# A three-stage kernel in split fp32 (attention, a rational expert layer, a gated layer): one operand of the rational moves to PSUM, weight casts of layer 1 move to GpSimd, and the order of work is ranked anew

## The chip, the core and the metric

The program runs on one core of a Trainium2 chip. A core has TensorE (matrix products, PE in the profile; its weight loads are PEld), VectorE (DVE), ScalarE (ACT), GpSimd (POOL), and SyncE (SP), which here issues every DMA. Each engine works through its own instructions in order. The metric is the device time in microseconds (us) of one execution. Before the change it is 624.5 us (median of three runs, 623.87 to 624.86).

## The reference, cut to what matters

```python
# q, k, v: 2 batches, 12 heads, 448 tokens, 64 per head; x has 896 tokens of 768
scores = where(causal, q @ k.T / 8, -1e9);  attn = softmax(scores);  x = attn @ v
# layer 1: 768 -> 2048 -> 768
h = x @ w_in
P = a[0] + a[1]*h + a[2]*h**2 + a[3]*h**3
Q = 1.0 + abs(b[0])*abs(h) + abs(b[1])*h**2
x = (P / (Q + 1e-6)) @ w_out
# layer 2: 768 -> 1536 -> 768
y = (sigmoid(x @ w_gate) * (x @ w_val)) @ w_out
```

The weights arrive as 64-bit floats. All of it is wanted at fp32 accuracy.

## The kernel before, in words

**Products.** Every large product is made of three passes in the type fp32r: a value is split into a rounded part ("hi") and the rest ("lo"), and hi·hi, hi·lo and lo·hi are summed in one PSUM bank. So each matrix multiplication of a tile of 128 x 448 (or 128 x 384) is a row of *units*, each of three matmuls (lines 228 to 230 for products with w_in, w_gate and w_val, lines 280 to 282 for products with w_out of layer 1, lines 340 to 342 for w_out of layer 2).

**Weights.** The generator `weight` (line 140) brings one *portion* of weights (128 x 768 values) through six stages: a DMA on SP, two ScalarE passes over the two halves of the 64-bit words (lines 152 and 156), a VectorE instruction that joins them to an fp32 value `val` (line 159, both inputs in SBUF), the cast of `val` to its hi part on ScalarE (line 165), and the subtraction that leaves the lo part on GpSimd (line 167). The buffers `raw` and `val` hold two portions each.

**Layer 1** is cut into four chunks c of 512 hidden values, for each of two batches b. `stage_in(c, b)` makes four tiles h{c}_{b}_{i} of six units each. Each tile is followed by `rational` (line 233): three ScalarE passes from the PSUM tile `ps` into the SBUF temporaries z, d and t (lines 238 to 240), three VectorE instructions (242 to 244), logarithm and exponential on ScalarE, which leave 1/Q in d (247, 248), three VectorE instructions (250 to 252), the cast to gh on ScalarE (254) and the subtraction to gl on GpSimd (256). The temporaries have two buffers each. `stage_out(c, b)` makes six tiles o{c}_{b}_{e} of four units, one unit for each of the chunk's four pairs gh, gl; VectorE adds each tile to a running sum in SBUF (line 290; in chunk 0 ScalarE copies it, line 288), and in the last chunk the sum is split again into xh and xl (294, 296).

**Layer 2** has six chunks: tiles gu and vu of six units, a gate (316 to 322), and 14 tiles z of two units per chunk, which VectorE adds up (line 350).

**PSUM.** The products go to banks of two pools, two banks in `ps_a` and, once the attention is over, six in `ps_b`. A tile takes the next bank of the ring and must wait until the tile that had it has been read.

**Order.** Nothing is scheduled on the chip. Each piece of work is a `Job` with an engine, an estimated cost, dependencies and a rank. `in_turn` (line 36) plays the jobs through with the estimated costs; whenever an engine is free in that play it takes, of the jobs that are ready, the one of lowest rank. The instructions of each engine are then written down in that order, for good. An engine that reaches an instruction too early waits in front of it, and everything behind it waits too. The numbers R_... (lines 519 to 524) shift the ranks of the attention's jobs, the dictionary `due` (line 616) gives the ranks of weights and follow-up work in the layers, and the list `order` (line 601) gives the order of the stages: in(0,0), out(0,0), in(0,1), in(1,0), out(0,1), in(1,1), out(1,0) and so on, so that an in-stage always stands between a stage's own in and out. The attention (12 pairs of heads) runs first on all engines; units of in(0,0), out(0,0) fill TensorE in between. The job `late` stands after the attention's last job: it frees the attention's memory and opens the second weight buffers and the pool `ps_b`.

Of the kernel before, what the change touches and what calls it, by code (L numbers as in the profile page):

```python
# [62 lines left out]

@with_exitstack
def tile_causal_attention__moe_rational__moe_glu(
# [535 lines left out]
    order = [("in", 0, 0), ("out", 0, 0), ("in", 0, 1)]  # L601
    for c in range(NCH):
        for b in range(B):
            if (c, b) != (0, 0):
                order.append(("out", c, b))
            if c + 1 < NCH:
                order.append(("in", c + 1, b))
    order += [("in2", 0, b) for b in range(B)]
    for c in range(NCH2):
        for b in range(B):  # L610
            order.append(("out2", c, b))
            if c + 1 < NCH2:
                order.append(("in2", c + 1, b))
# [1 line left out]
    due = {}
    pos = 1000.0
    for o in order:
        due[o] = pos
        pos += {
            "in": KC * NF * UNIT,  # L620
            "out": KC * NF * UNIT,
            "in2": 2 * KC * NF2 * UNIT,
            "out2": 2 * (ready[o[2] + 1] - ready[o[2]]) * NF2 * UNIT2,
        }[o[0]]
# [211 lines left out]
```

## Time and profile before

| | |
|---|---|
| median of three runs | 624.5 us |
| the profiled execution | 626.6 us, its span from the first to the last instruction 624.8 us |
| PE busy | 606.8 us, 97% of the span |
| DVE busy | 385.0 us, 62% |
| ACT busy | 382.5 us, 61% |
| POOL busy | 232.0 us, 37% |
| attention with its fill-in units | 0 to about 122.6 us |
| layer 1 from there, with the last sums | to about 355 us |
| layer 2 | the rest |

A share of the whole span is a mean over three stages that have different limits, so it does not tell what limits a stage. The windows of the trace tell that: the busy time of each engine in a stretch, and the clock that TensorE was granted in it (1.00 is full speed). A busy TensorE is not always a TensorE at its peak, since the ends of its matmuls are modelled; how many matmuls start in a stretch is the check on it.

### The profile page before, as it was taken

The numbers are of one execution on the slowest core, as the hardware profiler recorded it, in microseconds if no ns is written. First come the engines' busy times: TensorE is split into PE (matmuls) and PEld (weight loads), VectorE is DVE, ScalarE is ACT, GpSimd is POOL, SyncE is SP. The second block draws the span as 40 slices with busy tenths as digits, with TensorE's granted clock in tenths as the row PEclk, the third lists the DMA queues.
The fourth block names the chain that finished last, engine by engine and source line by source line (L and its number), as shares of the span: only waits on it lengthen the run. The fifth ranks groups of instructions, "written<-read, shape, count | busy, mean of one in ns | idle before, by whom it ended". The sixth has DMA issues, their size and how long they took to land.

```text
span 624.8 us, 8785 instructions
## 1 busy us (share of the span) xinstructions
PE 606.8 (97%) x3352; PEld 527.5 (84%) x3352; DVE 385.0 (62%) x659; ACT 382.5 (61%) x712; POOL 232.0 (37%) x155
## 2 busy tenths in 40 slices
PE   7998999999899999999996999999999999999997
PEld 5555566699799999999995999999999999999997
DVE  5776888838879999997896344435245245302314
ACT  6998988868877796878685276665516335121010
POOL 0332312245227444553446566435226135131110
PEclk9999999999999999999997999999999999999999
DMA  7643620153313341434050055434423232000004
GB/s 233 192 175 109 227 89 16 56 159 114 128 50 102 103 151 52 152 101 152 12 188 3 1 181 172 154 100 155 148 81 127 98 102 102 0 1 0 1 1 176
DMA packets 25641, 65.05 MB, mean 104 GB/s; under 512 B 1984, under 2 KB 3776, under 8 KB 25600
## 3 DMA queue, kind: packets, MB, share of 16 engines
q1 hardware_dynamic: 25600, 64.50, 31.6%
q8 instruction: 26, 0.43, 0.3%
q14 instruction: 15, 0.12, 0.1%
HBM read 61.74 MB, written 2.75 MB: 103 GB/s over the span
## 4 chain that ended last, share of the span: by engine, by line
PE 67%; DVE 19%; ACT 7%; issue 4%; DMA 2%; POOL 1%; DVEq 0%; POOLq 0%; ACTq 0%
PE vu L228 5%; PE vu L230 5%; PE gu L230 5%; PE gu L228 5%; PE gu L229 5%; PE vu L229 5%; PE z L340 5%; PE z L341 5%; PE z L342 5%; PE s L403 4%; DVE z_h L251 4%; PE p L443 4%; PE x L480 4%; DVE t_h L250 3%; DVE z_h L242 2%
## 5 line engine op out<-in xcount | busy, mean ns | idle before, releaser
L280 PE MATMUL o<-gh_h,oh_out 128*128 128x448 f32 x192 | 72.5, 378 | 4.6 <-ACT gh_h L254 4.6
L281 PE MATMUL o<-gl_h,oh_out 128*128 128x448 f32 x192 | 72.4, 377 | 4.1 <-POOL gl_h L256 4.1
L167 POOL TENSOR_TENSOR ol_out<-val_out,oh_out 128x768 fp32r<-128x768 f32 x28 | 55.2, 1983 | 48.3 <-ACT oh_out L165 40.2
L282 PE MATMUL o<-gh_h,ol_out 128*128 128x448 f32 x192 | 72.1, 375 | 0.0
L256 POOL TENSOR_TENSOR gl_h<-t_h,gh_h 128x448 fp32r<-128x448 f32 x32 | 43.2, 1349 | 76.8 <-ACT gh_h L254 62.9
L228 PE MATMUL h<-xh,wh_in 128*128 128x448 f32 x192 | 71.6, 373 | 0.0
L229 PE MATMUL h<-xl,wh_in 128*128 128x448 f32 x192 | 70.4, 367 | 1.0 <-POOL xl L501 1.0
L322 POOL TENSOR_TENSOR gl<-pr_u,gh 128x448 fp32r<-128x448 f32 x24 | 29.2, 1215 | 111.0 <-ACT gh L320 111.0
L230 PE MATMUL h<-xh,wl_in 128*128 128x448 f32 x192 | 70.1, 365 | 0.0
L318 DVE TENSOR_TENSOR pr_u<-sg_u,vu 128x448 f32<-128x448 f32 x24 | 14.8, 617 | 71.9 <-PE vu L230 59.6
L340 PE MATMUL z<-oh_out,gh 128*128 128x384 f32 x168 | 56.2, 334 | 0.0
L342 PE MATMUL z<-oh_out,gl 128*128 128x384 f32 x168 | 56.1, 334 | 0.0
L341 PE MATMUL z<-ol_out,gh 128*128 128x384 f32 x168 | 56.1, 334 | 0.0
L350 DVE TENSOR_TENSOR y<-y,z 128x384 f32<-128x384 f32 x70 | 37.9, 551 | 25.5 <-PE z L342 25.5
L425 ACT ACTIVATE e<-e,sc 112x112 f32<-112x112 f32 (+3 forms) x96 | 49.7, 523 | 6.1 <-DVE sc L411 6.1
L230 PE MATMUL gu<-xh,wl_gate 128*128 128x448 f32 x144 | 53.0, 368 | 0.0
L228 PE MATMUL vu<-xh,wh_val 128*128 128x448 f32 x144 | 53.0, 368 | 0.0
L229 PE MATMUL vu<-xl,wh_val 128*128 128x448 f32 x144 | 53.0, 368 | 0.0
L230 PE MATMUL vu<-xh,wl_val 128*128 128x448 f32 x144 | 53.0, 368 | 0.0
L229 PE MATMUL gu<-xl,wh_gate 128*128 128x448 f32 x144 | 53.0, 368 | 0.0
L228 PE MATMUL gu<-xh,wh_gate 128*128 128x448 f32 x144 | 52.9, 368 | 0.0
L411 DVE CUSTOM_DVE_ANT_0 e<-s,mask 112x112 f32<-112x112 f32 (+3 forms) x96 | 38.1, 444 | 20.6 <-PE p L443 10.5
(88 smaller groups left out, 1454.8 us busy)
## 6 DMA issues: line engine op xcount, KB each, us to landing
raw_out<-in_moe_w_out_dram SPq DMA_DIRECT2D x28, 768.0 KB, 4.3
raw_in<-in_moe_w_in_dram SPq DMA_DIRECT2D x16, 768.0 KB, 4.6
raw_gate<-in_moe_w_gate_dram SPq DMA_DIRECT2D x12, 768.0 KB, 4.4
raw_val<-in_moe_w_val_dram SPq DMA_DIRECT2D x12, 768.0 KB, 4.4
qk<-in_qk_dram SPq DMA_DIRECT2D x12, 448.0 KB, 5.8
v<-in_v_dram SPq DMA_DIRECT2D x12, 224.0 KB, 3.3
out_dram<-y SPq DMA_DIRECT2D x14, 192.0 KB, 1.8
a_sb<-in_moe_a_dram SPq DMA_DIRECT2D x1, 2.0 KB, 7.8
```

Source lines behind the costliest of these rows:

```text
L167: nc.gpsimd.tensor_tensor(lo, vf, hi, op=ALU.subtract)
L228: nc.tensor.matmul(ps, hi[:, c, fs], xh[:, c, bs], start=(c == 0), stop=False)
L229: nc.tensor.matmul(ps, hi[:, c, fs], xl[:, c, bs], start=False, stop=False)
L230: nc.tensor.matmul(ps, lo[:, c, fs], xh[:, c, bs], start=False, stop=(c == KC - 1))
L256: nc.gpsimd.tensor_tensor(gl, t, gh, op=ALU.subtract)
L280: nc.tensor.matmul(ps, hi[:, es], gh, start=(i == 0), stop=False)
L281: nc.tensor.matmul(ps, hi[:, es], gl, start=False, stop=False)
L282: nc.tensor.matmul(ps, lo[:, es], gh, start=False, stop=(i == NF - 1))
L340: nc.tensor.matmul(ps, gh[:, ms], hi[:, ns], start=(i == 0), stop=False)
L341: nc.tensor.matmul(ps, gh[:, ms], lo[:, ns], start=False, stop=False)
L342: nc.tensor.matmul(ps, gl[:, ms], hi[:, ns], start=False, stop=(i == NF2 - 1))
L425: nc.scalar.activation(e, e, AF.Exp, bias=d["sc"][:, t, j : j + 1], scale=-1.0, accum_out=d["sum"][:, t, j : j + 1])
```

## The change

Five things are done together.

1. In `rational`, d gets a pool of its own of two PSUM banks (`ps_d`) in the part after the attention, and the second of the last three VectorE instructions writes d in place of z. After that, each of the six VectorE instructions has at most one tensor input in SBUF. The temporaries t and z get three buffers in place of two; before `late`, d stays in SBUF with two.
2. The pool `ps_b` has four banks in place of six, so the ring of banks for products has six in place of eight.
3. For the weights of layer 1 (w_in and w_out, 32 portions) the cast to hi is done by GpSimd with a tensor_scalar in place of ScalarE's copy, in front of GpSimd's own subtraction. The weights of layer 2 keep ScalarE's cast.
4. The ranks are new: other shifts R_... in the attention; weights and follow-up work in the layers are ranked by the place of the unit that needs them.
5. Of the stage in2(0, 0), the first gu and vu tiles now stand after the third of the six tiles of out(3, 1), and the last three tiles of out(3, 1) behind them.

```diff
-    tmp = ctx.enter_context(tc.tile_pool(name="tmp", bufs=2))
+    tmp = ctx.enter_context(tc.tile_pool(name="tmp", bufs=3))
...
-        nc.scalar.copy(hi, vf)
+        if beside:
+
+            nc.gpsimd.tensor_scalar(hi, vf, 1.0, 1.0, op0=ALU.mult, op1=ALU.mult)
+        else:
+            nc.scalar.copy(hi, vf)
...
+    BY_POOL = ("in", "out")
...
-        pool = ps_a if nmm[0] % 8 < 2 else bank["b"]
+        pool = ps_a if nmm[0] % 6 < 2 else bank["b"]
...
-        d = tmp.tile([P, S], F32, tag="t2", name=f"d_{nm}")
+
+        if "d" in bank:
+            d = bank["d"].tile([P, 512], F32, tag="d", name=f"d_{nm}")[:, :S]
+        else:
+            d = tmp.tile([P, S], F32, tag="t2", name=f"d_{nm}", bufs=2)
...
-        nc.vector.scalar_tensor_tensor(z, z, one, d, op0=ALU.subtract, op1=ALU.mult)
-        nc.vector.scalar_tensor_tensor(t, z, 2.0, t, op0=ALU.add, op1=ALU.mult)
+        nc.vector.scalar_tensor_tensor(d, z, one, d, op0=ALU.subtract, op1=ALU.mult)
+        nc.vector.scalar_tensor_tensor(t, d, 2.0, t, op0=ALU.add, op1=ALU.mult)
...
-    R_TURN, R_R, R_X, R_W = -0.5, -8.5, 37.0, -4.0
-    R_MAX, R_COPY, R_INV, R_XN = -14.5, 2.0, -9.0, 10.0
-    R_EXP, R_ROUT = 4.25, -6.5
+    R_TURN, R_R, R_X, R_W = -11.0, -16.0, 34.0, -3.5
+    R_MAX, R_COPY, R_INV, R_XN = -14.5, -9.5, 7.0, 12.5
+    R_EXP, R_ROUT = 6.25, -42.5
...
-        bank["b"] = ctx.enter_context(tc.tile_pool(name="ps_b", bufs=6, space=PSUM))
+        bank["b"] = ctx.enter_context(tc.tile_pool(name="ps_b", bufs=4, space=PSUM))
+        bank["d"] = ctx.enter_context(tc.tile_pool(name="ps_d", bufs=2, space=PSUM))
...
         for m, (engine, cost) in enumerate(STAGES):
+            if m == 4 and key[0] in BY_POOL:
+                engine = "POOL"
...
-            rank = due["out", c, 0] + UNIT * i if c else W_AT + W_STEP * len(portions)
+            rank = ("out", c, 0, 0, "mm", i) if c else W_AT + W_STEP * len(portions)
...
-        ring = "b" if after and n_tiles[1] % 8 > 1 else "a"
-        deps = freed_by(ring, 6 if ring == "b" else 2) + ["late"] * after
+        ring = "b" if after and n_tiles[1] % 6 > 1 else "a"
+        deps = freed_by(ring, 4 if ring == "b" else 2) + ["late"] * after
...
-    def followed(key, stages, rank):
-
-        follow(key, stages, rank, n_tmp[-2:-1])
-        n_tmp.append((*key, "after", len(stages) - 1))
+    def followed(key, stages, rank, deps=()):
+
+        free = [(*k, "after", m) for k, m in n_tmp[-3:-2]]
+        free += [(*k, "after", 3) for k, _ in n_tmp[-2:-1]]
+        follow(key, stages, rank, [*free, *deps])
+        n_tmp.append((key, len(stages) - 1))
...
+    for n in range(2, len(ins)):
+
+        _run(stage_in(*ins[n]))
+        _run(stage_out(*ins[n - 1]))
+    woven("1110111", stage_in2(0, 0), stage_out(*ins[-1]))
```

What this does to two engines shows in their instructions. First GpSimd, from the second gl of stage in(1, 0) to the first gl of stage in(1, 1), where the four portions of w_out of chunk 1 are made (oh and ol are their hi and lo parts). Before:

```order
L256 TENSOR_TENSOR gl_h1_0_0_1770<-t_h1_0_1_1937,gh_h1_0_0_1769 128x448
L167 TENSOR_TENSOR ol_out1_0_2067<-val_out1_0_1836,oh_out1_0_2066 128x768
L167 TENSOR_TENSOR ol_out1_1_2076<-val_out1_1_2006,oh_out1_1_2075 128x768
L256 TENSOR_TENSOR gl_h1_0_2_1842<-t_h1_0_2_1993,gh_h1_0_2_1841 128x448
L167 TENSOR_TENSOR ol_out1_2_2108<-val_out1_2_2095,oh_out1_2_2107 128x768
L256 TENSOR_TENSOR gl_h1_0_2_1842<-t_h1_0_3_2033,gh_h1_0_2_1841 128x448
L167 TENSOR_TENSOR ol_out1_3_2155<-val_out1_3_2134,oh_out1_3_2154 128x768
L256 TENSOR_TENSOR gl_h1_1_0_2046<-t_h1_1_0_2128,gh_h1_1_0_2045 128x448
```

And now:

```order
L271 TENSOR_TENSOR gl_h1_0_0_1779<-t_h1_0_1_1905,gh_h1_0_0_1778 128x448
L172 TENSOR_SCALAR oh_out1_0_2067<-val_out1_0_1863 128x768
L176 TENSOR_TENSOR ol_out1_0_2068<-val_out1_0_1863,oh_out1_0_2067 128x768
L172 TENSOR_SCALAR oh_out1_1_2088<-val_out1_1_1993 128x768
L176 TENSOR_TENSOR ol_out1_1_2089<-val_out1_1_1993,oh_out1_1_2088 128x768
L271 TENSOR_TENSOR gl_h1_0_2_1850<-t_h1_0_2_2002,gh_h1_0_2_1849 128x448
L172 TENSOR_SCALAR oh_out1_2_2128<-val_out1_2_2094 128x768
L176 TENSOR_TENSOR ol_out1_2_2129<-val_out1_2_2094,oh_out1_2_2128 128x768
L271 TENSOR_TENSOR gl_h1_0_2_1850<-t_h1_0_3_2015,gh_h1_0_2_1849 128x448
L172 TENSOR_SCALAR oh_out1_3_2174<-val_out1_3_2143 128x768
L176 TENSOR_TENSOR ol_out1_3_2175<-val_out1_3_2143,oh_out1_3_2174 128x768
L271 TENSOR_TENSOR gl_h1_1_0_2061<-t_h1_1_0_2101,gh_h1_1_0_2060 128x448
```

Each of the four portions now has a cast on GpSimd in front of its subtraction: eleven instructions end with the first gl of in(1, 1) where there were seven behind the first row.

Second VectorE, at the last rationals of layer 1 (h3_1_2 and h3_1_3; the tiles o3_0_... are those of out(3, 0) and y1 is the running sum). Before, from the second half of h3_1_2:

```order
L250 SCALAR_TENSOR_TENSOR t_h3_1_2_3281<-t_h3_1_2_3281,a_sb_112,d_h3_1_2_3283 128x448
L251 SCALAR_TENSOR_TENSOR z_h3_1_2_3282<-z_h3_1_2_3282,one_115,d_h3_1_2_3283 128x448
L252 SCALAR_TENSOR_TENSOR t_h3_1_2_3281<-z_h3_1_2_3282,t_h3_1_2_3281 128x448
L290 TENSOR_TENSOR y1_0_1371<-y1_0_1371,o3_0_3_3333 128x448
L242 SCALAR_TENSOR_TENSOR z_h3_1_3_3343<-z_h3_1_3_3343,nb_114,d_h3_1_3_3344 128x448
L243 TENSOR_TENSOR t_h3_1_3_3342<-t_h3_1_3_3342,h3_1_3_3235 128x448
L244 SCALAR_TENSOR_TENSOR t_h3_1_3_3342<-t_h3_1_3_3342,a_sb_112,h3_1_3_3235 128x448
L290 TENSOR_TENSOR y1_0_1371<-y1_0_1371,o3_0_4_3358 128x448
L250 SCALAR_TENSOR_TENSOR t_h3_1_3_3342<-t_h3_1_3_3342,a_sb_112,d_h3_1_3_3344 128x448
L251 SCALAR_TENSOR_TENSOR z_h3_1_3_3343<-z_h3_1_3_3343,one_115,d_h3_1_3_3344 128x448
L252 SCALAR_TENSOR_TENSOR t_h3_1_3_3342<-z_h3_1_3_3343,t_h3_1_3_3342 128x448
L290 TENSOR_TENSOR y1_0_1371<-y1_0_1371,o3_0_5_3381 128x448
```

And now, from the first half of h3_1_3:

```order
L257 SCALAR_TENSOR_TENSOR z_h3_1_3_3301<-z_h3_1_3_3301,nb_114,d_h3_1_3_3302 128x448
L258 TENSOR_TENSOR t_h3_1_3_3300<-t_h3_1_3_3300,h3_1_3_3238 128x448
L259 SCALAR_TENSOR_TENSOR t_h3_1_3_3300<-t_h3_1_3_3300,a_sb_112,h3_1_3_3238 128x448
L305 TENSOR_TENSOR y1_0_1300<-y1_0_1300,o3_0_1_3295 128x448
L265 SCALAR_TENSOR_TENSOR t_h3_1_2_3266<-t_h3_1_2_3266,a_sb_112,d_h3_1_2_3268 128x448
L266 SCALAR_TENSOR_TENSOR d_h3_1_2_3268<-z_h3_1_2_3267,one_115,d_h3_1_2_3268 128x448
L267 SCALAR_TENSOR_TENSOR t_h3_1_2_3266<-d_h3_1_2_3268,t_h3_1_2_3266 128x448
L265 SCALAR_TENSOR_TENSOR t_h3_1_3_3300<-t_h3_1_3_3300,a_sb_112,d_h3_1_3_3302 128x448
L266 SCALAR_TENSOR_TENSOR d_h3_1_3_3302<-z_h3_1_3_3301,one_115,d_h3_1_3_3302 128x448
L267 SCALAR_TENSOR_TENSOR t_h3_1_3_3300<-d_h3_1_3_3302,t_h3_1_3_3300 128x448
L305 TENSOR_TENSOR y1_0_1300<-y1_0_1300,o3_0_2_3317 128x448
L305 TENSOR_TENSOR y1_0_1300<-y1_0_1300,o3_0_3_3339 128x448
```

The two rationals are now finished one right behind the other. Before, the sums of o3_0_3 and o3_0_4 stood ahead of the last instruction of h3_1_3; now those of o3_0_2 and o3_0_3 stand behind it. L266 writes d, where L251 wrote z.

## Rows read from the trace of the kernel before

**Rows 1.** Windows: start:end, length, busy us (instructions) by engine, PEclk granted clock, DMA.
```profile
0.00:40.00 40.00, 36.60 (x288) 22.90 (x289) 27.03 (x105) 32.60 (x87) 10.26 (x15) 1.00 0.64 203
40.00:80.00 40.00, 37.89 (x300) 23.09 (x300) 29.55 (x97) 37.17 (x101) 11.82 (x7) 1.00 0.48 163
80.00:122.60 42.60, 42.36 (x327) 27.36 (x327) 37.45 (x101) 36.30 (x95) 10.02 (x8) 1.00 0.19 57
122.60:167.00 44.40, 43.31 (x217) 39.70 (x214) 29.54 (x32) 34.48 (x54) 19.38 (x11) 1.00 0.43 143
167.00:184.00 17.00, 14.82 (x65) 13.00 (x64) 12.42 (x19) 13.75 (x26) 5.61 (x4) 0.90 0.07 26
184.00:245.00 61.00, 61.00 (x303) 56.54 (x302) 58.88 (x73) 51.75 (x83) 28.84 (x17) 1.00 0.34 110
...
332.00:346.00 14.00, 8.57 (x25) 6.59 (x24) 6.91 (x10) 5.09 (x10) 7.07 (x7) 0.63 0.00 0
346.00:600.00 254.00, 254.00 (x1298) 237.42 (x1298) 94.27 (x113) 103.57 (x154) 93.13 (x59) 1.00 0.27 87
```
**Rows 2.** Waits, 125 to 360 us: who <- for whom, total us, times, longest.
```profile
PE o L280 <- ACT gh_h L254: 4.3, 2, 2.9
...
PE o L281 <- POOL gl_h L256: 3.3, 3, 2.1
```
**Rows 3.** PE in order of time (start, length), first units of out(3, 1).
```profile
332.33 0.36 PE L280 MATMUL o<-gh_h,oh_out 128*128 128x448 f32 x1
334.77 0.48 PE L281 MATMUL o<-gl_h,oh_out 128*128 128x448 f32 x1 [2.08 <-POOL gl_h L256]
335.07 0.54 PE L282 MATMUL o<-gh_h,ol_out 128*128 128x448 f32 x1
338.49 0.74 PE L280 MATMUL o<-gh_h,oh_out 128*128 128x448 f32 x1 [2.88 <-ACT gh_h L254]
```
**Rows 4.** Two lines of the rational on DVE: ns, min/median/max.
```profile
L244 DVE SCALAR_TENSOR_TENSOR t_h<-t_h,a_sb,h x32: 679/681/683, 78.2 to 333.2; 128x448 f32<-128x448 f32 x32
...
L251 DVE SCALAR_TENSOR_TENSOR z_h<-z_h,one,d_h x32: 671/678/2272, 88.7 to 335.6; 128x448 f32<-128x448 f32 x32
```
**Rows 5.** DVE in order of time, 148 to 156 us.
```profile
148.92 2.16 DVE L252 SCALAR_TENSOR_TENSOR t_h<-z_h,t_h 128x448 f32<-128x448 f32 x1
151.00 2.60 DVE L159 SCALAR_TENSOR_TENSOR val_in<-raw_in 128x768 uint32<-128x768 uint32 x1
```
**Rows 6.** POOL in order of time, the same stretch.
```profile
148.30 4.49 POOL L167 TENSOR_TENSOR wl_in<-val_in,wh_in 128x768 fp32r<-128x768 f32 x2 [12.67 <-ACT wh_in L165]
```
**Rows 7.** Groups on DVE, 130 to 345 us: count, busy us, mean ns, idle before.
```profile
L251 DVE SCALAR_TENSOR_TENSOR z_h<-z_h,one,d_h 128x448 f32<-128x448 f32 x28 | 28.7, 1024 | 0.0
L242 DVE SCALAR_TENSOR_TENSOR z_h<-z_h,nb,d_h 128x448 f32<-128x448 f32 x28 | 27.9, 998 | 5.5 <-ACT d_h L239 5.4
L252 DVE SCALAR_TENSOR_TENSOR t_h<-z_h,t_h 128x448 f32<-128x448 f32 x28 | 26.0, 929 | 1.0
L250 DVE SCALAR_TENSOR_TENSOR t_h<-t_h,a_sb,d_h 128x448 f32<-128x448 f32 x28 | 25.3, 903 | 9.8 <-ACT d_h L248 9.3
```
**Rows 8.** Lines 167 and 256 on POOL, 159 on DVE: ns, min/median/max.
```profile
L167 POOL TENSOR_TENSOR ol_out<-val_out,oh_out x28: 1820/1852/2589, 53.8 to 549.7; 128x768 fp32r<-128x768 f32 x28
...
L256 POOL TENSOR_TENSOR gl_h<-t_h,gh_h x32: 1129/1208/1915, 93.2 to 338.5; 128x448 fp32r<-128x448 f32 x32
...
L159 DVE SCALAR_TENSOR_TENSOR val_out<-raw_out x28: 947/958/2604, 50.5 to 530.0; 128x768 uint32<-128x768 uint32 x28
```
**Rows 9.** Groups on POOL (whole span) and ACT (to 122.6 us): busy us, mean ns.
```profile
L120 POOL MEMSET mask<- 112x448 f32 x1 | 0.5, 475 | 0.0
masks.py:199 POOL TENSOR_SCALAR_AFFINE_SELECT ident<-ident 128x128 f32<-128x128 f32 x1 | 0.3, 293 | 0.0
...
masks.py:197 POOL MEMSET ident<- 128x128 f32 x1 | 0.2, 204 | 0.3 <-POOLq L823 0.3
...
L165 ACT CAST wh_in<-val_in 128x768 fp32r<-128x768 f32 x4 | 3.3, 836 | 0.6 <-DVE val_in L159 0.5
```

More of the change, by code (lines that the diff above doesn't have):

```diff
@@ L61, in in_turn, with _run @@
         yield job
+def _run(g):
+    while not _spent(g):
+        pass
 @with_exitstack
@@ L181, in cols @@
         return [
-            weight(lambda cs=cs: dst(cs), sv[:, cs], f"{key[0]}{key[1]}_{key[2]}_{cs.start}") for cs in parts
+            weight(lambda cs=cs: dst(cs), sv[:, cs], f"{key[0]}{key[1]}_{key[2]}_{cs.start}", key[0] in BY_POOL)
+            for cs in parts
         ]
@@ L595, in late @@
         ypools[1] = ctx.enter_context(tc.tile_pool(name="y_b", bufs=1))
-        bank["b"] = ctx.enter_context(tc.tile_pool(name="ps_b", bufs=6, space=PSUM))
+        bank["b"] = ctx.enter_context(tc.tile_pool(name="ps_b", bufs=4, space=PSUM))
+        bank["d"] = ctx.enter_context(tc.tile_pool(name="ps_d", bufs=2, space=PSUM))
     job("late", "", 0.0, [k for k in J if k != "ab"], 0, late)
[L601 to L613, printed above, removed]
-    UNIT, UNIT2 = 0.615, 0.52
[L615 to L624, printed above, removed]
-    STAGES = [("SP", 4.0), ("ACT", 0.92), ("ACT", 0.9), ("DVE", 1.2), ("ACT", 0.84), ("POOL", 1.9)]
+    UNIT, UNIT2 = 0.615, 0.52
+    STAGES = [("SP", 4.0), ("ACT", 0.92), ("ACT", 0.9), ("DVE", 1.3), ("ACT", 0.84), ("POOL", 2.0)]
     portions = []
@@ L640, in portion @@
             r = rank
-            if rank < 1000:
+            if not isinstance(rank, tuple):
                 r = rank - 4 if m == 0 else rank + R_W
@@ L669, in weights_out2 @@
             free = [("out", NCH - 1, 1, KC - 1, "mm", NF - 1) if c < 2 else ("out2", c - 2, ready[B] - 1, 1, "mm", NF2 - 1)]
-            portion((*key, 0), rows(wt, key, w_out2, c * NF2 + i), free, due["out2", c, 0] + UNIT2 * i)
+            portion((*key, 0), rows(wt, key, w_out2, c * NF2 + i), free, ("out2", c, 0, 0, "mm", i))
     tiles = {}
@@ L675, in tile_causal_attention__moe_rational__moe_glu @@
     n_tiles = [0, 0]
+    at = {"end": 1000.0}
     def products(key, make):
@@ L685, in matmuls @@
         unit = (*key, "mm", u)
+        at[unit] = at["end"]
+        at["end"] += cost
     def place(key, read):
@@ L735, in stage_out @@
                 matmuls(key, i, deps + [("out", c, i, 0, 5), ("in", c, b, i, "after", 5)], UNIT, out1_tile)
-            follow(key, stages, due["out", c, b] + 15)
+            follow(key, stages, at["end"] + R_SUM)
+            yield
     def stage_in2(c, b):
@@ L760, in stage_out2 @@
                     matmuls(key, i, deps + [("out2", c, i, 0, 5), *gs], UNIT2, out2_tile)
-                follow(key, stages, due["out2", c, b] + 10)
+                follow(key, stages, at["end"] + R_SUM)
+                yield
     weights_in(0)
@@ L775, in tile_causal_attention__moe_rational__moe_glu, with woven @@
         weights_out2(c)
-    for name, *at in order:
-        {"in": stage_in, "out": stage_out, "in2": stage_in2, "out2": stage_out2}[name](*at)
+    def woven(pattern, *stages):
+        for p in pattern:
+            _spent(stages[int(p)])
+        for g in stages:
+            _run(g)
+    _run(stage_in(0, 0))
+    _run(stage_out(0, 0))
+    _run(stage_in(0, 1))
+    ins = [(c, b) for c in range(NCH) for b in range(B)]
+    for n in range(2, len(ins)):
+        _run(stage_in(*ins[n]))
+        _run(stage_out(*ins[n - 1]))
+    woven("1110111", stage_in2(0, 0), stage_out(*ins[-1]))
+    _run(stage_in2(0, 1))
+    for c in range(NCH2):
+        for b in range(B):
+            _run(stage_out2(c, b))
+            if c + 1 < NCH2:
+                _run(stage_in2(c + 1, b))
+    for j in J.values():
+        if isinstance(j.rank, tuple):
+            j.rank = at[j.rank]
     latest = {}
```

19 lines of the change are left out of this document (11 added, 8 removed).

## The prediction

> **What bounds the kernel now.** The table of busy shares says TensorE, 97%. The windows, read next, say where the other 3% lie [rows 1]: TensorE has no idle time from 346 to 600 us (254.00 of 254.00), so nothing in layer 2 can be won from the other engines. It idles 3.40 + 2.11 + 0.24 us in the attention, 1.09 us between 122.6 and 167, 2.18 us between 167 and 184 and 5.43 us between 332 and 346. In the last two stretches the granted clock is also down, to means of 0.90 and 0.63, which is part of the time at 1.2 in place of 2.4 GHz, just behind the waits. So count matmuls: undisturbed layer 1 starts 303 in 61 us, one per 0.201 us. In 167 to 184 that would be 84 where 65 are seen, 19.4 x 0.201 = 3.9 us lost; in 332 to 346 it would be 69.5 for 25, 9.0 us lost. These 12.9 us hold the waits and the slow clock behind them.
>
> The waits name gh and gl, the results of the rational, at the first units of an out-stage [rows 2]; in out(3, 1) the second unit's gl is 2.08 us late and the next gh again 2.88 us [rows 3]. Why they are late shows on VectorE: it is busy 58.88 of 61 us in 184 to 245 [rows 1], so in layer 1 it has no reserve. And part of that is waiting inside instructions: line 244, which has one input in PSUM, takes 679 to 683 ns in all 32 cases, line 251, all in SBUF, 671 to 2272 [rows 4]. At 148.92 an SBUF-only instruction takes 2.16 us and the next 2.60 [rows 5], while GpSimd runs two subtractions through 4.49 us [rows 6]. Each long VectorE instruction lies over a GpSimd one.
>
> **The change, part by part.** *The operand in PSUM.* Lines 242, 250, 251 and 252 are the four that now get one input from PSUM. In 130 to 345 us they took 28.7 + 27.9 + 26.0 + 25.3 = 107.9 us for 28 rationals [rows 7]; at the 0.68 us of line 244 they would take 4 x 28 x 0.68 = 76.2. That is 31.7 us less, 1.13 us a rational, and for the 8 of a chunk 9.1 of 61 us. VectorE goes from 58.9 to 49.8 us a chunk. No instruction of before writes PSUM from VectorE or ScalarE, or lets ScalarE read a temporary there; with 0.68 as the price of line 244, I bound the six accesses of a rational by a tenth of a microsecond each way, 5 us a chunk over two engines, and take nothing: both then have over 9 us free.
>
> The Trainium skill ("SBUF — State Buffer", Who interferes with whom) says that a VectorE instruction with two SBUF inputs contends with a GpSimd instruction that reads SBUF, the later one waiting for the whole of the other, and one with at most one SBUF input does not. The trace agrees for line 244. But by the same rule line 164, the join of the weights, still has two SBUF inputs, and GpSimd now reads SBUF longer; that is the second rival.
>
> Line 164 itself: its median was 0.958 us and its worst 2.604 [rows 8], so between 0 and 8 x 1.65 = 13.2 us a chunk may be added. GpSimd's share rises by 6.7 of 61 us (below), so I take 2 us, near the median. VectorE then stands at 52 of 61 us.
>
> *The lateness that this removes.* Out(3, 1) lacked its results by 2.1 and then 2.9 us, out(0, 1) by 2.2 us in all (its idle time). A chunk of two in-stages saves 9 us on VectorE before such a point, and the last two rationals of layer 1 now have fewer sums in front of them. So I take both losses as gone whole, 3.9 + 9.0, and of the 1.09 us at 122.6 half. What is late next there is the weights, through GpSimd.
>
> *The cast on GpSimd.* The trace has no such cast. From below: a memset, which reads nothing, takes 475 ns for 448 columns and 204 for 128 [rows 9], 0.85 ns a column, so 0.75 us for 768. From above: the subtraction of 768 columns with two inputs, 1.85 us, or 2.59 where it waited [rows 8]. The nearest row is the select with one input and one output, 293 ns for 128 columns; with 640 more at 0.85 ns that is 0.84 us, which I take. The Trainium skill ("GPSIMD Engine Reference", Engine selection) calls one-input work on GpSimd roughly line-rate, and its 1.03 cycles per element at 1.2 GHz would be an estimated 0.66 us and change the sum by nothing. No run here shows it yet.
>
> GpSimd then has 28.8 + 8 x 0.84 = 35.6 us of 61. The path that counts: casts of w_out of the next chunk may begin when an out-stage ends, and behind them, in GpSimd's order, stand their subtractions and two gl. To the fourth unit of the next out-stage TensorE has 24 + 3 units of three matmuls, 27 x 0.604 = 16.3 us. GpSimd needs 4 x (0.84 + 1.85) + 2 x 1.21 = 13.2 us: 3.1 us to spare. With a cast of 1.85 it needs 17.2, and TensorE waits 0.9 us at each of out(1, 0), out(2, 0) and out(3, 0). I take 1 us in all for new waits of this and other kinds, with 0 and 8 as ends (8: casts of 1.85 and three waits of 0.9, each with a slow clock behind it that costs as much again as before, and 3 us for the banks below).
>
> ScalarE loses 8 x 0.84 = 6.7 us a chunk, 51.75 to 45; it was not what TensorE waited for in layer 1 except behind VectorE.
>
> *Six banks for products.* An h tile holds a bank until the third VectorE instruction has read it. In layer 1 VectorE now has time for that. In layer 2 a tile z is made in 1.0 us and VectorE waits there for TensorE, whose busy time had no hole. Two banks fewer are 2 us of cover less; I take zero there.
>
> *The attention.* ScalarE is the fullest engine beside TensorE, 37.17 of 40 us in 40 to 80 [rows 1]. Eight casts of 0.836 us go [rows 9], 6.7 us. The most that can come back is the idle time of TensorE, 5.75 us to 122.6, of which I leave the 3.40 us up to 40 us to the start-up; 2.35 remain, plus what the modelled ends hide. The other way, each GpSimd cast now stands ahead of an xl that a unit needs, 2.7 us with its subtraction; two such places would cost 5. I take 2 us gained, with -5 and +5 as ends, since the ranks are all new.
>
> *The boundary to layer 2.* TensorE had no idle time from 346 us on, so moving three tiles of out(3, 1) behind the first gu and vu wins nothing by itself. It gives the sums of out(3, 0) less time before gu needs them, three out tiles, 36 x 0.201 = 7.2 us, where one sum, cast and subtraction take under 3. Zero.
>
> **The sum.** 3.9 + 9.0 + 0.5 + 2 - 1 = 14.4 us. The profiled execution took 626.6 us (span 624.8, 1.8 around it); 626.6 - 14.4 = 612.2. It lay 2.1 us above the median of 624.5, so the forecast on the median's scale is 610.1, given as 610.
>
> **The rivals.** *One: only part comes back.* The weights or the banks keep TensorE waiting at some out-stages: the gain shrinks by the 8 us of the upper end, to about 617. For it speaks that GpSimd's cast has no row; against it the 3.1 us to spare.
>
> *Two: line 164 takes it all.* If each join meets a GpSimd instruction whole, 13.2 us a chunk come on top of 49.8, VectorE stands at 63 of 61 and the results are late as before: 624, no change. Against it: the median of 0.958 with GpSimd at 47%; it would have to be always the worst case.
>
> *Three: GpSimd becomes the bound, slower.* If a cast and its subtraction take p together, TensorE waits 4p + 2.4 - 16.3 us at three out-stages. At 332 us, idle time of 5.4 cost 9.0 in all, a factor of 1.65. The gain of 14 is eaten when 3 x 1.65 x (4p - 13.9) = 14, at p = 4.2 us. With both at the longest seen for the subtraction, p = 5.2: 4p - 13.9 = 6.9, 34 us lost, 644. At p = 4.6, 22 us lost, 632. For it: GpSimd works in order, and a cast that waits for its buffer holds up the gl behind it. Against it: p by rows is 2.7, and 3.7 if a cast costs a subtraction.
>
> *Four: the attention gains more than I take,* up to its +5 and without new waits: 606.
>
> **Chances.** The forecast, 605 to 614: 0.58. Rival one, 614 to 622: 0.20. Rival two: 0.05. Rival three: 0.10. Rival four, under 605: 0.07. The likeliest case's own range is 605 to 614. The range with 8 in 10 reaches into rivals four and one: 604 to 621. A measurement here tells 0.2%, 1.2 us, from no change: faster 0.85, same 0.05, slower 0.10.
>
> **What would show it.** In the profile after: lines 257 and 265 to 267 with maxima near 0.68 us; VectorE near 52 of 61 us in the middle of layer 1; no wait of line 295 or 296 over 1 us and a granted clock of 1.00 in all windows of layer 1; the cast of line 172 near 0.84 us; ScalarE under 35 of 40 us in 40 to 80. I am wrong if line 172 takes over 1.9 us, if TensorE waits at out(1, 0) to out(3, 0) for ol, or if the attention ends after 123 us.

## The result, and the profile after

The changed kernel takes 614.7 us (median of four runs, 614.2 to 615.48) where the kernel before took 624.68 beside it: a ratio of 0.9832, interval 0.9815 to 0.9848. The forecast was 610, its range 604 to 621. A second series of the unaltered kernel, told below, gave 609.82 us. That one program has two times, and what tells them apart in a trace, is the main finding of the study.

The windows of the profiled execution (614.51 us, span 612.5), with the columns of [rows 1]:

```profile
0.00:40.00 40.00, 36.69 (x281) 22.87 (x283) 27.87 (x105) 31.12 (x91) 13.78 (x19) 1.00 0.63 201
40.00:80.00 40.00, 40.00 (x323) 24.81 (x321) 32.86 (x99) 34.21 (x95) 16.43 (x13) 1.00 0.52 176
80.00:122.60 42.60, 41.54 (x316) 27.29 (x317) 37.38 (x100) 34.80 (x90) 9.84 (x8) 1.00 0.14 42
122.60:167.00 44.40, 44.40 (x222) 39.87 (x219) 32.03 (x43) 33.15 (x54) 28.43 (x20) 1.00 0.45 148
167.00:184.00 17.00, 17.00 (x84) 15.43 (x83) 11.46 (x17) 14.95 (x28) 8.77 (x7) 1.00 0.16 47
184.00:245.00 61.00, 61.00 (x297) 55.41 (x296) 47.95 (x70) 39.42 (x66) 35.88 (x27) 1.00 0.35 116
...
332.00:346.00 14.00, 14.00 (x70) 12.71 (x69) 2.30 (x4) 5.11 (x7) 4.60 (x4) 1.00 0.01 2
346.00:600.00 254.00, 254.00 (x1304) 237.97 (x1303) 92.97 (x117) 102.71 (x151) 91.59 (x58) 1.00 0.28 90
```

TensorE has no hole from 122.6 to 600 us, and the granted clock is 1.00 in every row. The 84 and 70 matmuls in the two short windows are those that the prediction counted for an undisturbed layer 1. But in 184 to 245, full in both kernels, there are 297 matmuls now and 303 in [rows 1]: the same matmuls at the same clock start more slowly. (A window also counts the two matmuls that already run at its start, so a mean taken from the count is a little under the spacing of the starts: 61/303 is 0.2013 us, the spacing 0.2027.)

The first units of out(3, 1), in the columns of [rows 3], have no wait:

```profile
328.00 0.37 PE L295 MATMUL o<-gh_h,oh_out 128*128 128x448 f32 x1
328.21 0.37 PE L296 MATMUL o<-gl_h,oh_out 128*128 128x448 f32 x1
328.42 0.37 PE L297 MATMUL o<-gh_h,ol_out 128*128 128x448 f32 x1
328.62 0.37 PE L295 MATMUL o<-gh_h,oh_out 128*128 128x448 f32 x1
```

The groups on VectorE, 130 to 345 us, which answer to [rows 7], and the joins of the weights (line 164):

```profile
L266 DVE SCALAR_TENSOR_TENSOR d_h<-z_h,one,d_h 128x448 f32<-128x448 f32 x28 | 19.1, 683 | 0.0
...
L257 DVE SCALAR_TENSOR_TENSOR z_h<-z_h,nb,d_h 128x448 f32<-128x448 f32 x28 | 18.9, 676 | 13.4 <-ACT d_h L254 13.4
L265 DVE SCALAR_TENSOR_TENSOR t_h<-t_h,a_sb,d_h 128x448 f32<-128x448 f32 x28 | 18.9, 676 | 4.9 <-ACT d_h L263 4.9
L164 DVE SCALAR_TENSOR_TENSOR val_out<-raw_out 128x768 uint32<-128x768 uint32 x14 | 18.0, 1283 | 4.2 <-POOL ol_out L176 2.3 <-ACT raw_out L161 1.9
L267 DVE SCALAR_TENSOR_TENSOR t_h<-d_h,t_h 128x448 f32<-128x448 f32 x28 | 17.5, 624 | 1.0
...
L164 DVE SCALAR_TENSOR_TENSOR val_in<-raw_in 128x768 uint32<-128x768 uint32 x10 | 14.4, 1448 | 8.4 <-POOL wl_in L176 4.8 <-ACT raw_in L161 3.6
```

The four lines take 74.4 us where they took 107.9. The joins before, in the same stretch:

```profile
L159 DVE SCALAR_TENSOR_TENSOR val_out<-raw_out 128x768 uint32<-128x768 uint32 x14 | 17.0, 1223 | 0.0
L159 DVE SCALAR_TENSOR_TENSOR val_in<-raw_in 128x768 uint32<-128x768 uint32 x10 | 13.8, 1383 | 10.8 <-ACT raw_in L156 7.5 <-POOL wl_in L167 3.3
```

The cast on GpSimd (ns, min/median/max):

```profile
L172 POOL TENSOR_SCALAR wh_in<-val_in x16: 832/838/1547, 18.2 to 217.3; 128x768 fp32r<-128x768 f32 x16
L172 POOL TENSOR_SCALAR oh_out<-val_out x16: 832/837/850, 49.0 to 308.2; 128x768 fp32r<-128x768 f32 x16
```

**Where the time went.** Both kernels start the same 2520 product matmuls in layers 1 and 2. The time that each stretch of them takes, from one matmul's start to another's (us, worked out from the starts in the traces; "again" is the second series):

```
matmuls        place                       before   after   again
to no. 100     start, attention             128.2   125.5   125.3
100 to 288     in(0,1) to first stall        38.1    38.9    38.1
288 to 360     first stall [rows 2]          18.9    14.9    14.6
360 to 1080    middle of layer 1            145.9   148.8   145.9
1080 to 1152   out(3,1) [rows 3]             24.0    14.9    14.6
1152 to 2519   layer 2                      265.8   265.8   265.2
```

After against before: the attention gives 2.75, the two stalls 4.0 and 9.1, and the undisturbed stretches take 0.75 + 2.9 back. In the second series those stretches cost what they cost before.

### The profile page after: what moved, and what is told of

The parts are those of the page before. It is cut to its first block, busy times and chain, and to the rows that moved or that the text cites. A ratio compares the mean times of both kernels' runs of the same rounds, so it can differ in the third digit from the quotient of the medians.

```text
span 612.5 us, 8782 instructions
## 1 busy us (share of the span) xinstructions
PE 604.6 (99%) x3352; PEld 524.1 (86%) x3352; DVE 357.9 (58%) x659; ACT 356.8 (58%) x680; POOL 256.6 (42%) x187
## 3 DMA queue, kind: packets, MB, share of 16 engines
HBM read 61.74 MB, written 2.75 MB: 105 GB/s over the span
## 4 chain that ended last, share of the span: by engine, by line
PE 97%; DVE 2%; issue 0%; ACT 0%; DVEq 0%
PE h L239 7%; PE o L295 7%; PE h L240 6%; PE h L241 6%; PE o L296 6%; PE o L297 6%; PE vu L239 5%; PE vu L241 5%; PE gu L239 5%; PE gu L241 5%; PE vu L240 5%; PE gu L240 5%; PE z L355 5%; PE z L356 5%; PE z L357 5%; PE s L418 4%
## 5 line engine op out<-in xcount | busy, mean ns | idle before, releaser
L271 POOL TENSOR_TENSOR gl_h<-t_h,gh_h 128x448 fp32r<-128x448 f32 x32 | 41.9, 1310 | 79.3 <-ACT gh_h L269 79.2
L295 PE MATMUL o<-gh_h,oh_out 128*128 128x448 f32 x192 | 71.2, 371 | 0.0
L297 PE MATMUL o<-gh_h,ol_out 128*128 128x448 f32 x192 | 70.6, 368 | 0.0
L296 PE MATMUL o<-gl_h,oh_out 128*128 128x448 f32 x192 | 70.6, 368 | 0.0
L176 POOL TENSOR_TENSOR ol_out<-val_out,oh_out 128x768 fp32r<-128x768 f32 x28 | 53.5, 1918 | 29.0 <-ACT oh_out L174 27.6
L164 DVE SCALAR_TENSOR_TENSOR val_out<-raw_out 128x768 uint32<-128x768 uint32 x28 | 34.0, 1215 | 26.4 <-ACT raw_out L161 23.9
```

Of the source, the lines that this page charges most:

```text
L176: nc.gpsimd.tensor_tensor(lo, vf, hi, op=ALU.subtract)
L271: nc.gpsimd.tensor_tensor(gl, t, gh, op=ALU.subtract)
L295: nc.tensor.matmul(ps, hi[:, es], gh, start=(i == 0), stop=False)
L296: nc.tensor.matmul(ps, hi[:, es], gl, start=False, stop=False)
L297: nc.tensor.matmul(ps, lo[:, es], gh, start=False, stop=(i == NF - 1))
```

## The experiments

All are edits of the changed kernel, but for e4. e1 to e4 ran beside runs of the kernel before with a median of 625.72 us.

**e1: d back in SBUF**, the order of instructions unaltered.

```diff
-        if "d" in bank:
+        if False:
```

> The kernel after, with d kept in SBUF (two buffers) and nothing else changed: the order of every engine is the same, and the ring of product banks stays at six. Theory (VectorE's waits inside instructions with two SBUF inputs made the results late): lines 257, 265, 266 and 267 reach 2 us again, mean 0.9 to 1.0 us where they take 0.68 with d in PSUM, TensorE waits at out(0, 1) and out(3, 1) again, and the time is 620 to 627 us. Rival (the new ranks and the third buffers of t and z ended the lateness, the place of d matters little): no wait over 1 us, 614 to 616.5 us.

Measured: 624.59 us, ratio 0.9981 (0.9962 to 1.0001); the profiled execution, 622.53 us, was the fastest of ten. The gain is gone. VectorE's groups, 130 to 345 us:

```profile
L265 DVE SCALAR_TENSOR_TENSOR t_h<-t_h,a_sb,d_h 128x448 f32<-128x448 f32 x28 | 32.3, 1155 | 0.5 <-ACT d_h L263 0.5
L267 DVE SCALAR_TENSOR_TENSOR t_h<-d_h,t_h 128x448 f32<-128x448 f32 x28 | 28.2, 1006 | 1.0
L257 DVE SCALAR_TENSOR_TENSOR z_h<-z_h,nb,d_h 128x448 f32<-128x448 f32 x28 | 26.4, 943 | 3.3 <-ACT d_h L254 3.3
L266 DVE SCALAR_TENSOR_TENSOR d_h<-z_h,one,d_h 128x448 f32<-128x448 f32 x28 | 25.6, 916 | 1.0
```

TensorE's waits, 122 to 360 us:

```profile
PE o L295 <- DVE t_h L259: 4.2, 3, 1.5
PE o L297 <- POOL ol_out L176: 1.2, 1, 1.2
```

With the same order, line 265 takes a mean of 1155 ns with d in SBUF and 676 in PSUM. Its median is 681 ns in SBUF too (676 in PSUM), so the place costs nothing by itself; the long instances, up to 2001 ns, make the mean. The rule of the Trainium skill ("SBUF — State Buffer", Who interferes with whom) that the prediction weighed agrees with these 1155 and 676 ns.

The four lines take 112.5 us, against 107.9 in [rows 7] and 74.4 with d in PSUM. But the time is not lost where the theory had it. From no. 288 to 360 and from 1080 to 1152 the stretches cost 16.0 and 16.5 us, 1.2 and 1.6 more than in the changed kernel; the middle of layer 1 costs 155.2, 6.4 more, though most of it ran at 202.7 ns a start. The largest waits, 4.2 us, are those of a fifth tile in out(1, 0), out(1, 1) and out(2, 0) for a bank that an h tile holds until line 259 has read it: with a ring of six, a late VectorE is felt there first. Whether the casts on GpSimd would pay with d in SBUF was not run.

**e2: all casts on ScalarE.**

```diff
-    BY_POOL = ("in", "out")
+    BY_POOL = ()
```

> The kernel after, with the casts of layer 1's weights on ScalarE as before; the order is played through anew with that. Theory: layer 1 stays without waits, since VectorE has its reserve, and only the attention is slower, by the casts that ScalarE gets back: the 100th product matmul starts 1 to 4 us later, 616 to 619 us. Rival (GpSimd's casts relieve layer 1 too): waits at out-stages, over 620 us.

Measured: 621.0 us, ratio 0.9936 (0.9917 to 0.9955), slower than expected. The executions fall in two groups, six at 620.0 to 621.1 and four at 622.6 to 623.7; the profiled one, 623.66, is of the upper. TensorE's waits, 122 to 360 us:

```profile
PE o L295 <- ACT gh_h L269: 3.5, 1, 3.5
PE o L296 <- POOL gl_h L271: 1.3, 2, 1.1
PE o L295 <- ACT y L303: 1.3, 1, 1.3
```

A window at the attention's end:

```profile
125.00:133.00 8.00, 4.87 (x13) 4.00 (x14) 4.29 (x6) 5.85 (x8) 5.31 (x3) 0.57 0.64 198
```

Matmul no. 100 starts at 134.3, 8.8 us later than in the changed kernel (1 to 4 were expected), and the end is 9.4 later. So what the cast on GpSimd is worth under the new shifts is won up to there, not in layer 1, where one wait of 1.3 us comes back: the rational of in(0, 0) is late at the attention's end, and the clock falls (0.57 in the mean) behind the wait of 3.5 us. That a full ScalarE is the reason is not shown: in 40 to 80 it is busy 33.63 of 40 us here and 34.21 in the changed kernel.

**e3: the shifts R_... of before**, and the rank of the attention's scores.

```diff
-    R_TURN, R_R, R_X, R_W = -11.0, -16.0, 34.0, -3.5
-    R_MAX, R_COPY, R_INV, R_XN = -14.5, -9.5, 7.0, 12.5
-    R_EXP, R_ROUT = 6.25, -42.5
+    R_TURN, R_R, R_X, R_W = -0.5, -8.5, 37.0, -4.0
+    R_MAX, R_COPY, R_INV, R_XN = -14.5, 2.0, -9.0, 10.0
+    R_EXP, R_ROUT = 4.25, -6.5
...
-                rank - 37.5,
+                rank - 29.5,
```

> The kernel after, with the shifts R_ and the rank of the scores of the kernel before, so that only the attention is ranked as before. Theory (ScalarE's eight casts are what the attention gained by): the 100th product matmul starts within 1 us of the kernel after, 613.5 to 616 us. Rival (the shifts gained it): it starts 2 to 4 us later, 617 to 619 us.

Measured: 614.63 us, ratio 0.9829 (0.9808 to 0.985), the time that the theory expected. The total misleads. In its trace no. 100 starts at 127.8, 2.3 us later than in the changed kernel, and a wait in layer 1 is back:

```profile
PE h L239 <- DVE t_h L259: 1.4, 1, 1.4
```

Yet by no. 1080 it is level (328.1 against 328.0): its matmuls start every 202.7 ns where those of the changed kernel start every 206.7. Against the second series, which has 202.7 too, the old shifts lose 4.2 us in the trace. So the start is as late as the rival had it, and the theory's time came of the other pitch.

The four traces together say more of the attention than each run alone. No. 100 starts at 128.2 with the old shifts and the casts on ScalarE (the kernel before, which differs in other parts too), at 127.8 with the old shifts and the casts on GpSimd (e3), at 134.3 with the new shifts and the casts on ScalarE (e2), and at 125.5 with both new. Neither part has the attention's gain by itself: in these traces the new shifts gain only with the casts on GpSimd, and the casts gain little without them.

**e4: the kernel before with d in PSUM** and six banks for products. The ranks are those of before, but the play with six banks writes down another order on VectorE, ScalarE and GpSimd; TensorE's is the same.

```diff
-        pool = ps_a if nmm[0] % 8 < 2 else bank["b"]
+        pool = ps_a if nmm[0] % 6 < 2 else bank["b"]
...
-        nc.vector.scalar_tensor_tensor(z, z, one, d, op0=ALU.subtract, op1=ALU.mult)
+        nc.vector.scalar_tensor_tensor(d, z, one, d, op0=ALU.subtract, op1=ALU.mult)
...
```

> The kernel before with d in two PSUM banks and the ring at six in place of eight, and nothing else: casts, buffers of t and z, ranks and stages as before. Theory: the waits at out(0, 1) and out(3, 1) go, 12.9 us in the profile of before; less 4 us if layer 1 then runs at a matmul start every 206.7 ns as after in place of 202.7: 611 to 617 us. Rival (ranks and buffers did it): 621 to 625 us.

Measured: 616.86 us, ratio 0.9879 (0.9848 to 0.991). Without the other parts of the change, d in PSUM gives 8.9 us in the medians, 11.2 in the traces (e4's profiled execution, 615.47, is the fastest of four). It shows at the two places: no. 288 to 360 takes 15.4 us where before took 18.9, and 1080 to 1152 takes 15.8 where before took 24.0. The matmuls of layer 1 start every 202.7 ns, so the theory's 4 us for the other pitch did not come in. What the new order of the three engines adds is not told apart. Small waits of TensorE stay:

```profile
PE o L284 <- POOL gl_h L259: 2.0, 3, 0.8
PE o L283 <- ACT gh_h L257: 0.4, 1, 0.4
```

**e5: no weave at the boundary**, all six tiles of out(3, 1) first.

```diff
-    woven("1110111", stage_in2(0, 0), stage_out(*ins[-1]))
+    _run(stage_out(*ins[-1]))
+    _run(stage_in2(0, 0))
```

> The changed kernel with all six tiles of out(3, 1) in front of the first gu and vu, as before the change; nothing else differs. Theory (the weave is worth nothing, since the sums of out(3, 0) are ready in time either way): 614 to 616 us, no wait of TensorE over 0.5 us between 325 and 350 us, granted clock 1.00 there. Rival (the weave hides the last rational of in(3, 1) and carries part of the 9 us won at this place): waits of the first units of out(3, 1) for gl or gh of 1 us or more come back, with a lower granted clock behind them, and the time is 618 to 624 us.

Measured: 609.94 us, ratio 0.9769 (0.9722 to 0.9816), with executions at 609.58, 609.72, 610.15 and one at 615.15. No wait of TensorE in layer 1. Both expectations missed the time, and a program with two times 5 us apart had to be explained. In the profiled execution matmuls of layer 1 start every 202.7 ns. Its span is 607.6 us, that of the second series of the changed kernel: at the same pitch the weave is worth nothing, as the theory and the prediction had it.

**p1: extra matmuls of ten widths**, overwritten at once, in front of stages.

```diff
+    SHIFT = [256, 64, 384, 128, 320, 192, 416, 288, 96, 352]
...
+            nc.tensor.matmul(ps[:, :k], hi[:, 0, fs], xh[:, 0, b * S : b * S + k], start=True, stop=True)
```

> The changed kernel with one extra matmul in front of the first tile of every in-stage and every pair of gate tiles, into the same bank and overwritten at once; its width runs through 256, 64, 384, 128, 320, 192, 416, 288, 96 and 352 columns, 19 of them in all. Theory (TensorE at full granted clock has two steady pitches for the 128x448 matmuls, one start per 202.7 or per 206.7 ns, and which of them it keeps is set by how the last disturbance left it): behind some of the widths the pitch is 202.7 ns and stays so until the next one; where half of layer 1 runs so the extra matmuls, some 4 us in all, are about paid back: 612 to 619 us. Rival one (the pitch belongs to the stage, by its operands or by what else runs then): 206.7 ns throughout layer 1 and 2 as in the changed kernel, 618 to 620 us. Rival two (the pitch follows what VectorE, ScalarE and GpSimd do, not TensorE's own past): it changes at places that have nothing to do with the extra matmuls.

Measured: 611.17 us (one run), a little under the 612 expected, with 19 matmuls more than the changed kernel. Windows between three of them; 416 columns stand at 296.0, 288 columns at 333.4:

```profile
267.00:295.90 28.90, 28.90 (x144) 26.78 (x143) 21.82 (x34) 20.76 (x34) 11.04 (x7) 1.00 0.34 109
297.50:333.00 35.50, 35.50 (x174) 32.24 (x173) 25.38 (x36) 25.31 (x42) 23.84 (x19) 1.00 0.31 104
335.00:355.00 20.00, 20.00 (x100) 18.53 (x99) 5.55 (x6) 6.85 (x10) 11.17 (x8) 1.00 0.09 22
```

The mean spacing of the starts is 202.7 ns up to the 416 columns, 206.7 behind them, and 202.7 again behind the 288. Behind the z tiles it is 202.7 after every width but 352 and 384; in the changed kernel it is always 206.7 there. So TensorE has two steady pitches, and its own last disturbance sets which. Both rivals fall: the pitch changes inside layer 1, and at the extra matmuls.

**p2: one narrow matmul (64 columns) in front of in(0, 1)**, an edit like p1's.

> The changed kernel with a single extra matmul of 64 columns, in front of in(0, 1), the first in-stage behind the attention, overwritten at once. Theory (a pitch of TensorE that is kept until the next disturbance): layer 1 runs at 202.7 ns a matmul from 134 us to the first z tile at about 371, in place of 206.7: some 1150 matmuls by 4 ns, 4.6 us; 610 us. Rival one (the pitch comes back to 206.7 by itself, or the 64 columns leave it as it was): 614 to 615.5 us. Rival two (the 4 ns are given back as waits for VectorE, which then has less time per chunk): 202.7 ns, but waits of over 1 us in layer 1 and 612 to 615 us.

Measured: 610.02 us (609.83 to 610.24), ratio 0.9746 (0.9717 to 0.9776). As expected, but it proves less than it seems: in this trace the pitch is 202.7 ns ahead of the narrow matmul already.

**after_again and p4: the changed kernel unaltered, and with 416 columns** at p2's place.

> The changed kernel once more, unaltered, beside the next one. Theory (the pitch of TensorE is settled by how the last disturbance, here the end of the attention, happens to fall, and may differ between executions): each execution lies either near 610 us (202.7 ns in layer 1) or near 614.5 (206.7 ns), none between 611 and 613. Rival (the pitch is fixed by the program): 614 to 615.5 us in all, as before. Which of the two the profiled execution has is read from its trace: by the starts of matmuls in 184 to 245 us, 302 or more at 202.7 ns, 297 at 206.7.

> The changed kernel with one extra matmul of 416 columns in front of in(0, 1), where a matmul of 64 columns stood in an earlier run. Theory (a narrow matmul in front leaves the pitch at 202.7 ns, a wide one does not set it there, as 416 columns before in(3, 1) turned it to 206.7): 206.7 ns from 135 us on, 614.5 to 616 us. Rival (any extra matmul at this place does it, or none does and the end of the attention decides): near 610 us.

Measured: 609.82 us unaltered (609.29 to 610.14; ratio 0.9754, 0.9737 to 0.9771), and 614.86 with 416 columns (one execution of four at 610.5; ratio 0.9817, 0.9782 to 0.9851). A window of the unaltered kernel:

```profile
184.00:245.00 61.00, 61.00 (x303) 56.54 (x302) 48.38 (x72) 39.56 (x67) 36.99 (x27) 1.00 0.36 116
```

The same with 416 columns, where the trace has 202.7 ns up to the extra matmul and 206.7 from there:

```profile
184.00:245.00 61.00, 61.00 (x297) 55.41 (x296) 47.65 (x71) 39.86 (x67) 35.83 (x27) 1.00 0.36 113
```

The unaltered kernel has 303 matmuls here, where it had 297 in the first series. So 4.9 us between two series of one program are the pitch. All eight executions lie near 610 or 614.5, none between; the one at 610.5 has no trace, but by its time the wide matmul does not always bring the slower pitch. In e5 and here the same program showed both times within one series on one chip, so the chip alone does not settle the pitch.

**p3 and p3_again: eleven narrow matmuls**, in front of in(0, 1) and of the ten in-stages of layer 2 behind z tiles, without the weave.

```diff
...
+        if first:
+            nc.tensor.matmul(ps[:, :64], hi[:, 0, fs], xh[:, 0, b * S : b * S + 64], start=True, stop=True)
...
```

> The changed kernel with all six tiles of out(3, 1) ahead of the first gu and vu, and with eleven extra matmuls of 64 columns, overwritten at once: in front of in(0, 1), and in front of the first gate tile of each of the ten in-stages of layer 2 that follow z tiles. Theory: besides layer 1, the gu and vu tiles of five chunks, 720 matmuls, run at 202.7 in place of 206.7 ns: 2.9 us, less eleven times some 0.03 us; 607 us. Rival (behind z tiles the pitch is 206.7 whatever stands between): 610 us. It would be the fastest version if the theory holds.

> The version with eleven matmuls of 64 columns once more, unaltered, in more rounds. Theory (the narrow matmul behind the attention's end sets 202.7 ns whichever pitch it finds, and those in layer 2 do so behind the z tiles): every execution between 608 and 610 us, none near 614. Rival (the pitch of an execution is settled elsewhere, and the four earlier executions all had the faster one by luck): some executions 4 to 5 us above the others.

Measured: 608.99 us (608.37 to 609.56), ratio 0.9731 (0.9704 to 0.9757); again 608.17 (607.93 to 608.7, five runs), ratio 0.9728 (0.9715 to 0.9742). The first lies between the theory's 607 and the rival's 610. No execution is near 614. TensorE in the first of the two, where the pitch was 206.7 ahead of the narrow matmul:

```profile
134.90 0.37 PE L297 MATMUL o<-gh_h,oh_out 128*128 128x448 f32 x1
135.10 0.37 PE L298 MATMUL o<-gl_h,oh_out 128*128 128x448 f32 x1
135.31 0.37 PE L299 MATMUL o<-gh_h,ol_out 128*128 128x448 f32 x1
135.51 0.19 PE L239 MATMUL h<-xh,wh_in 128*128 128x64 f32 x1
135.54 0.44 PE L241 MATMUL h<-xh,wh_in 128*128 128x448 f32 x1
135.83 0.36 PE L242 MATMUL h<-xl,wh_in 128*128 128x448 f32 x1
136.02 0.36 PE L243 MATMUL h<-xh,wl_in 128*128 128x448 f32 x1
```

Ahead of it starts come every 0.20 or 0.21 us, one in a mean of 206.7 ns; behind it the mean is 202.7. The start behind the narrow one's successor comes 0.29 us later, not 0.20, so each costs some 0.1 us, not 0.03; in layer 2 the traces give 1.5 us for ten, not the 2.6 expected (no. 1152 to 2519: 263.7 us against 265.2 in after_again). This is the fastest version. Where the attention's end left the slower pitch, the narrow matmul ended it, in the one trace that has this, and none of the nine executions shows the slower time.

**e6: each cast on GpSimd three times.**

```diff
+            for _ in range(3):
+                nc.gpsimd.tensor_scalar(hi, vf, 1.0, 1.0, op0=ALU.mult, op1=ALU.mult)
```

> The changed kernel with each cast on GpSimd done three times over. GpSimd's time per chunk rises by 16 times 0.84, 13.4 of 61 us, to about 49. By the working of the third rival a cast and its subtraction then take p = 3 x 0.84 + 1.85 = 4.4 us, and TensorE waits 4 x 4.4 + 2.4 - 16.3 = 3.7 us for ol at each of out(1, 0), out(2, 0) and out(3, 0): 18 us lost with the slow clock behind the waits, 632 us. Rival (the portions are spread over more time than that working allows, since w_in's come between): waits for ol under 1 us, 614 to 618 us.

Measured: 631.6 us (one run), waits of TensorE, 124 to 360 us:

```profile
PE o L296 <- POOL oh_out L173: 5.3, 3, 2.3
PE o L298 <- POOL ol_out L177: 3.7, 3, 1.2
```

The third rival's mechanism is real, and its place is right: at out(1, 0), out(2, 0) and out(3, 0). The time is right for a mixed reason. The three places cost 5.6 + 4.2 + 3.6 = 13.4 us against the second series, not 18, the start up to no. 100 another 5.7 and the stretches from there to no. 360 another 2.4, which were not in the sum. And TensorE waits first for oh_out, the cast itself, where the working had only ol.

## Why the prediction was right, point by point

- **The two stalls.** Taken as 3.9 + 9.0, measured 4.0 + 9.1 after against before. Reading a stall as matmuls that did not start, the slow clock behind it included, gave both sizes. The cause is the operand's place: e4 shows it at these two places, 18.9 to 15.4 and 24.0 to 15.8 us, and e1, with the order unaltered, shows that the gain goes without it, though e1 loses its time elsewhere.
- **The attention and its boundary.** Taken as 2 + 0.5, measured 2.75. The split was a little off: the boundary gave its whole 1.09 us, not half (44.40 of 44.40 us busy), and TensorE's idle time up to 122.6 us fell from 5.75 to 4.37. ScalarE stands at 34.21 of 40 us, as the "under 35" said, but the reason given, eight casts less on ScalarE, does not carry the gain by itself: with the old shifts it moves no. 100 by 0.4 us only (128.2 before, 127.8 in e3). So the size of this term is in part luck. One of the prediction's own signs of being wrong came up, the attention ending after 123 us. Its last matmuls, before:

```profile
120.79 2.11 PE L480 MATMUL x<-pt,v 112*64 112x448 f32 x16
```

  And after:

```profile
121.89 2.11 PE L495 MATMUL x<-pt,v 112*64 112x448 f32 x16
```

  They end at 124.0 where they ended at 122.9. It was no loss: 94 product matmuls have started by then in place of 81.
- **VectorE.** Forecast 52 of 61 us, measured 47.95. The four lines came out as taken (0.62 to 0.68 us). Mis-sized was the term for the joins, 2 us more a chunk, reckoned from their median of 0.958. Their waits were already in the 58.88 of before: 24 joins took 17.0 + 13.8 = 30.8 us there and take 18.0 + 14.4 = 32.4 now, 0.5 us more for the eight of a chunk, and nowhere near the 13.2 of rival two. The rest is the window's cut: it holds four instructions of the rationals fewer and one sum more (70 instructions, before 73).
- **GpSimd.** The cast was taken as 0.84 us and takes 0.838, closer than a sum from a select and a memset, with bounds of 0.75 and 1.85, could promise. The estimate of 0.66 us from the 1.03 cycles per element of the Trainium skill ("GPSIMD Engine Reference", Elementwise — side-by-side cycle accounting) was too low by a fifth. The chunk was taken as 35.6 us and takes 35.88, but the window holds nine casts and one subtraction of ol more, and the gl take less (means of 1.27 us, before 1.39). No wait for ol came, and e6 shows that the margin was real and not wide.
- **ScalarE.** Forecast 45, measured 39.42. The window has 66 instructions where it had 83: nine casts fewer, and by the new order two passes over weights, five passes of the rationals and a copy. The accesses to d in PSUM were taken as nothing; the exponential became 0.05 us faster (last section).
- **New waits** were taken as 1 us. There were none, which leaves rival one without its mechanism; yet its time, 614 to 622, is where the first series lay, 0.7 us outside the likeliest case's own 605 to 614.
- **What the sum left out.** TensorE's undisturbed rate was taken as the same in both kernels, one start per 0.201 us. In the first series it was 206.7 ns, which took back 3.6 us of the 15.9 that the other terms gave: 12.3 in the spans. With the pitch of before, in the second series, the median is 609.82 against the 610 forecast. The before side adds a caution: its profiled execution was 2.1 us above its median, so spans (17.2 us apart with the second series) say more than medians (15.6). Against those 17.2 the sum of 14.4 was 2.8 short: 0.8 on the two stalls, 1 on new waits, 0.4 on the attention and 0.5 in layer 2. That 609.82 stands so near 610 is in part luck.

Not shown: why the end of the attention leaves one pitch in some executions and the other in others, and what inside TensorE the two pitches are. The kernel before has one trace only; whether its executions (623.74 to 628.48 in the runs beside e1 to e4) differ by pitch is open.

## What to carry to other kernels

Where VectorE and GpSimd run side by side, count a VectorE instruction's SBUF inputs: one of them moved to PSUM gave 8.9 us without the other parts, and left VectorE room beside a GpSimd that has more to do. Where two parts change together, look at each without the other: here the moved casts alone did little for the attention, and the new shifts alone did harm. Before a difference of under 1% is put down to an edit, count matmuls in an undisturbed window of both traces: two kernels can differ by TensorE's pitch alone, and e3 looked like no difference for that reason. Size a stall by the starts that are missing, not by the wait.
